# An attention and two expert layers on one core: the first pair's hash projections and first scores in smaller operations, and a new order

## The chip, the core and the metric

One core of a Trainium2 chip runs one program. The metric is the device time of one execution in microseconds (us), shown as the median of a few runs. The engines are TensorE (PE; its weight loads are PEld), VectorE (DVE), ScalarE (ACT), GpSimd (POOL) and SyncE (SP), which only issues DMAs. Each engine takes its instructions in the order in which they stand in its own queue.

## What is computed

The reference is an attention with hashed masks (batch 2, 8 heads, 768 positions, 64 columns per head), whose output passes through two feed-forward networks without any routing.

```
q_bits = (q @ proj > 0); k_bits = (k @ proj > 0)        # six bits each
mask   = bucket(q_bits) == bucket(k_bits)
scores = where(mask, q @ k.T / 8, -1e9)
attn   = exp(scores - max) / (sum + 1e-9);  x = attn @ v
h = x @ w_in;   x = (h * sigmoid(h)) @ w_out            # 1536 x 512 -> 2048 -> 512
a = x @ w1; b = x @ w2;  out = ((a * b) @ w3) @ wo2     # 512 -> 1024 -> 1024 -> 512
```

## The kernel before

The 16 heads are worked off as eight pairs, each pair on 128 partitions (one head on each half). For a pair the kernel multiplies the transposed q and k by the hash matrix (the projections), turns the results into sign bits on VectorE, and adds the bits to the scores as a fourth product with a large weight, so that entries outside the bucket fall far below the others. For each block of 128 rows of a head it then takes the row's peak on VectorE, the exponential on ScalarE, transposes the probabilities, and multiplies them with V. Meanwhile the weights of the two networks are loaded as split words, joined, and divided into a rounded part and a rest ("pieces", helper `piece`); three matmuls of such parts stand for one of full precision. The product of w3 and wo2 (L961) is made during the attention too. After the attention come the layers' matmuls (L1124, L1244, L1288).

The first pair is made in another way than the others (`lone` in the code). Its q and k arrive in four quarters of 384 columns (`raw["k", 0]` and so on, L540). Each is rounded (helper `scaled`, L348 to L352) and the rest is taken by a subtraction (`rest`, L592 on VectorE, L355 on POOL). The projections (`project`, L623) and signs (`sign`, L629) are made per half of the columns, q and k together; the weighted marks of k (`mark_k`, L679) follow, one operation per half. The scores (`scores_lone`, L767) of one block of rows of both heads are one operation of four passes:

```
passes = [("qhi", "khi"), ("qlo", "khi"), ("qhi", "klo"), ("bits", "marks")]
for p, (x, y) in enumerate(passes):
    ...
    for g in range(2):
        for side in range(2):
            ...
            nc.tensor.matmul(out=area(side * NQ + i)[:, g, :HF], lhsT=lhs[k, qs],
                             rhs=rhs[k, g * HF:g * HF + HF], start=(p == 0), stop=(p == 3))
```

Peaks of all pairs are L771, exponentials L777. The first pair's probabilities are turned by TensorE (L800), moved into their tile (`carry`, L806 on ScalarE or L808 on VectorE), and summed up with V (L842); the other pairs' are turned by VectorE (L818) and weighed by L876, and their scores are L755. At a pair's end the rows' sums are raised (L906, POOL or VectorE), inverted (L910, VectorE) and turned (L913). L535 are filler matmuls, whose result nobody reads.

What stands in which engine's queue is not left to a scheduler. Every operation is recorded with its possible engines, its predecessors and the buffers that it takes and gives back. Two tables at the head of the file then set everything: `ORDER` lists the operations' numbers in the order in which they are issued, and `ON` has a letter for the engine of each (P, A, D, G, S).

```
for n, e in zip(ORDER, ON):
    o = self.ops[n]
    ...
    for pool, key in o.take:
        self.held[key] = pool, self.free[pool].pop(0)
    o.emit(ENGINES[e])
```

Buffers are taken from their pools in this order, so an order also decides which buffer an operation gets. The costs and due times that the calls of `op` carry are not used when the program is built.

Of the kernel before, what the change touches and what calls it, by code (L numbers as in the profile page):

```python
# [12 lines left out]
ALU = mybir.AluOpType  # L13
# [215 lines left out]
def dve(n):  # L229
    return (n + 72) / 0.96  # L230
# [33 lines left out]
class Plan:  # L264
# [10 lines left out]
    def op(self, on, emit, deps=(), due=0.0, take=(), give=(), size=0, port=False, kind=None, tiled=False):  # L275


        self.ops.append(Op(on, emit, deps, take, give))
        return self.ops[-1]
# [1132 lines left out]
```

## Time and profile before

| what | us |
|---|---|
| median of 3 runs | 693.67 |
| lowest and highest run | 688.51, 696.32 |
| the profiled execution | 689.96 |
| its span, first to last instruction | 688.2 |
| TensorE busy in it | 668.1 |
| VectorE, ScalarE, POOL busy | 517.4, 381.5, 259.5 |

The profile is one execution. A busy engine is not always a fast one: the granted clock (PEclk) says at which share of full speed TensorE was let run. In rows of instructions the first figures are the start and the duration in us, and the square bracket names how long the engine stood idle before it and what ended that.

### The profile page before, as it was taken

What the parts mean: (1) busy time and instruction counts of PE and PEld (TensorE: products, weight loads), DVE (VectorE), ACT (ScalarE), POOL (GpSimd) and SP (SyncE); (2) the same over time, 40 slices, a digit from 0 to 9 for tenths busy, and PEclk for the clock granted to TensorE, in tenths of its full rate; (3) what the DMA queues carried; (4) which work ended last, traced back from release to release, by engine and by line L of the source; (5) the groups of instructions that cost most, each with busy time, mean ns of one, the idle gap of its engine ahead of it and who ended that gap; (6) DMA issues with size and microseconds to landing.
All of it is one profiled execution on the core that took longest, in us unless ns stands there. A gap on an engine that the chain in (4) does not pass through costs nothing.

```text
span 688.2 us, 13741 instructions
## 1 busy us (share of the span) xinstructions
PE 668.1 (97%) x5542; PEld 544.8 (79%) x5542; DVE 517.4 (75%) x736; ACT 381.5 (55%) x707; POOL 259.5 (38%) x268
## 2 busy tenths in 40 slices
PE   8899999998998998999999999999999999999997
PEld 6557787877787887888888888888887788888886
DVE  5889989978899867667796976778868575545465
ACT  5788778757778665467653543643545454322220
POOL 5468986777686220674200220211223144000000
PEclk9899999999999999999999999999999999999999
DMA  6465665446435444012530121110310012000004
GB/s 198 132 216 156 205 169 159 140 134 209 129 104 133 116 105 129 1 61 63 177 129 1 61 92 47 61 47 1 122 47 28 20 61 77 1 0 16 0 16 168
DMA packets 21551, 64.16 MB, mean 93 GB/s; under 512 B 3312, under 2 KB 4848, under 8 KB 21040
## 3 DMA queue, kind: packets, MB, share of 16 engines
q1 hardware_dynamic: 21488, 63.30, 29.8%
q8 instruction: 43, 0.70, 0.4%
q14 instruction: 20, 0.16, 0.1%
HBM read 55.19 MB, written 5.29 MB: 88 GB/s over the span
## 4 chain that ended last, share of the span: by engine, by line
PE 86%; DVE 6%; ACT 3%; issue 3%; DMA 1%; SPq 0%; ACTq 0%; DVEq 0%
PE more L1288 20%; PE more L1124 16%; PE more L1244 9%; PE acc L1288 9%; PE score L755 7%; PE acc L876 5%; PE acc L961 5%; PE acc L1124 4%; PE acc L1244 4%; DVE st L771 2%; PE turn L876 2%; ACT P L777 2%; PE acc L842 1%; PE score L767 1%; DVE pt L818 1%
## 5 line engine op out<-in xcount | busy, mean ns | idle before, releaser
L1124 PE MATMUL more<-y,piece 128*128 128x512 f32 x498 | 126.3, 390 | 0.6 <-DVE y L355 0.3
L1124 PEld LDWEIGHTS more<-y,piece 128*128 128x128 f32 x498 | 93.0, 188 | 21.7 <-DVE y L355 0.8
L777 ACT ACTIVATE P<-score,st 128x768 f32<-128x768 f32 x92 | 82.6, 899 | 37.4 <-DVE st L771 33.0
L771 DVE TENSOR_REDUCE st<-score 128x1 f32<-128x770 f32 x92 | 85.5, 943 | 13.1 <-PE score L755 10.1
L1288 PE MATMUL more<-gh,piece 128*128 128x512 f32 x256 | 88.5, 390 | 0.0
L818 DVE STREAM_TRANSPOSE pt<-P 128x768 f32<-128x768 f32 x84 | 79.9, 963 | 4.9 <-ACT P L777 4.7
L1307 DVE SCALAR_TENSOR_TENSOR X<-more,X 128x512 f32<-128x512 f32 x84 | 57.0, 686 | 35.0 <-PE more L1288 34.6
L1244 PE MATMUL more<-x,piece 128*128 128x512 f32 x252 | 65.1, 390 | 0.0
L876 PE MATMUL turn<-pt,V 32*64 32x193 f32 x1344 | 61.0, 325 | 3.3 <-issue 3.3
L876 PE MATMUL acc<-pt,V 32*64 32x193 f32 x1344 | 60.9, 325 | 2.4 <-issue 1.7
L876 PEld LDWEIGHTS acc<-pt,V 32*64 32x64 f32 x1344 | 50.5, 130 | 7.5 <-issue 6.2
L1288 PEld LDWEIGHTS more<-gh,piece 128*128 128x128 f32 x256 | 48.1, 188 | 10.2 <-DVE kraw L1190 0.3
L1244 PEld LDWEIGHTS more<-x,piece 128*128 128x128 f32 x252 | 47.2, 188 | 10.1 <-DVE X L1307 0.3
L755 PE MATMUL score<-ka,qa 128*128 128x384 f32 x168 | 46.9, 360 | 4.4 <-ACT P L777 4.3
L876 PEld LDWEIGHTS turn<-pt,V 32*64 32x64 f32 x1344 | 47.0, 130 | 4.6 <-issue 4.6
L352 POOL TENSOR_SCALAR piece<-x 128x512 fp32r<-128x512 f32 x35 | 24.1, 691 | 70.6 <-PE more L1288 29.4
L961 PE MATMUL acc<-piece,piece 128*128 128x512 f32 x192 | 50.1, 397 | 0.0
L1288 PE MATMUL more<-gl,piece 128*128 128x512 f32 x128 | 49.8, 389 | 0.0
L405 DVE SCALAR_TENSOR_TENSOR x<-x,x 128x512 uint32<-128x512 uint32 x57 | 43.3, 762 | 3.0 <-ACT x L390 2.3
L755 PE MATMUL score<-kb,qb 76*128 76x384 f32 x168 | 43.3, 338 | 0.0
L755 PEld LDWEIGHTS score<-ka,qa 128*128 128x128 f32 x168 | 28.3, 188 | 17.5 <-ACT P L777 9.5
L1288 PE MATMUL more<-piece,gh 128*128 128x512 f32 x132 | 40.6, 389 | 0.0
(229 smaller groups left out, 1426.1 us busy)
## 6 DMA issues: line engine op xcount, KB each, us to landing
raw<-in_w SPq DMA_DIRECT2D x27, 512.0 KB
raw<-in_wo SPq DMA_DIRECT2D x21, 512.0 KB
raw<-in_win SPq DMA_DIRECT2D x15, 512.0 KB
V<-in_v SPq DMA_DIRECT2D x14, 384.0 KB
invb<-inverse SPq DMA_DIRECT2D x16, 192.0 KB
out<-X SPq DMA_DIRECT2D x11, 256.0 KB
qraw<-in_qT SPq DMA_DIRECT2D x7, 384.0 KB
kraw<-in_kT SPq DMA_DIRECT2D x7, 384.0 KB
```

Source lines behind the costliest of these rows:

```text
L352: engine[e].tensor_scalar(out=dst, in0=src, scalar1=by, scalar2=1.0, op0=ALU.mult, op1=ALU.mult)
L405: engine[e].scalar_tensor_tensor(out=u32(x), in0=u32(x), scalar=3, in1=u32(t), op0=ALU.logical_shift_left, op1=ALU.bitwise_or)
L755: nc.tensor.matmul(out=sc[:, g, :HF], lhsT=lhs[:k, qs], rhs=rhs[:k, g * HF:g * HF + HF], start=(k == 128), stop=(k != 128),)
L771: nc.vector.tensor_reduce(out=plan[uk("st")][:, 0:1], in_=area()[:, :, :HF + 1], op=ALU.max, axis=AX.XY, negate=True)
L777: nc.scalar.activation(out=plan[uk("P")], in_=area()[:, :, :HF], func=AF.Exp, bias=s[:, 0:1], accum_out=plan[key("sums")][:, par * NQ + i: ...
L818: nc.vector.transpose(plan[mine][:, :, 32 * i:32 * i + 32], plan[uk("P")].rearrange("p g (b i) -> p (g b) i", i=32))
L876: nc.tensor.matmul(out=to[a][64 * side:64 * side + 64, :GW + 1], lhsT=V[rows_, c, side], rhs=plan[key(f"pt{side}")][rows_, c, :GW + 1], st ...
L961: nc.tensor.matmul(out=plan[key + ("ps",)], lhsT=w[:, a, k], rhs=r[:, c], start=(k == 0 and n == 0), stop=(k == 7 and n == 2),)
L1124: nc.tensor.matmul(out=plan[bk[b]], lhsT=w[:, a], rhs=y, start=(opens and j == 0 and m == 0), stop=(j == 1 and m == 2), skip_group_check=True)
L1244: nc.tensor.matmul(out=plan[key], lhsT=w[:, a], rhs=x, start=(k == 0 and n == 0), stop=(k == 3 and n == 2))
L1288: nc.tensor.matmul(out=plan[key], lhsT=a, rhs=x, start=(f == 0 and n == 0), stop=(f == 1 and n == 2))
L1307: nc.vector.scalar_tensor_tensor(out=dst, in0=plan[key], scalar=by, in1=dst, op0=ALU.mult, op1=ALU.add)
```

## The change

The first pair's projections are now made per half of the columns and per source: k's two matmul calls, then q's two, each with a sign operation on its own 64 partitions, in place of one projection of four calls and one sign on 128 partitions. The marks of k wait for k's sign alone. The first scores (block 0 of both heads) are two operations: three passes that wait for the rounded parts and rests, and the marked pass, which waits for the marks and for q's sign; the other blocks' scores wait for q's sign too. 2,939 recorded operations become 2,944. `ORDER` and `ON` are new as a whole; numbered alike, their last 1,307 entries are the same as before.

```
 SOON = 60
 ORDER = [
-    32, 34, 36, 35, 33, 44, 40, 38, 42, 827, 841, 0, 37, 18, 19, 1, 46, 48, 14, 13, 45, 39, 43, 47, 49, 51, 52, 54, 55,
+    32, 34, 33, 36, 35, 832, 846, 0, 37, 17, 1, 42, 43, 44, 40, 833, 834, 835, 46, 30, 50, 10, 52, 4, 45, 38, 39, 41, 47,
...
-            def project(e, f=f, fs=fs, key=key):
-                for t in range(4):
-                    nc.tensor.matmul(
-                        out=plan[key(f"z{f}")][32 * t:32 * t + 32, :HF], lhsT=ptl[:, t % 2],
-                        rhs=plan[key("qk"[t // 2] + "raw")][:, fs], start=True, stop=True,
-                    )
...
+            for w, nm in enumerate("kq"):
+                rows_ = slice(64 - 64 * w, 128 - 64 * w)
+
+                def project(e, f=f, fs=fs, nm=nm, key=key):
+                    for t in (0, 1) if nm == "q" else (2, 3):
+                        nc.tensor.matmul(
+                            out=plan[key(f"z{f}")][32 * t:32 * t + 32, :HF], lhsT=ptl[:, t % 2],
+                            rhs=plan[key(nm + "raw")][:, fs], start=True, stop=True,
+                        )
+
+                def sign(e, f=f, fs=fs, rows_=rows_, key=key, of_pair=part_of_pair):
+                    nc.vector.tensor_scalar(
+                        out=of_pair("bits")[rows_, fs], in0=plan[key(f"z{f}")][rows_, :HF], scalar1=0.0, scalar2=sel[rows_, 0:1],
+                        op0=ALU.is_gt, op1=ALU.is_equal,
                     )
...
-                    mine.append(op({"DVE": 420, "POOL": pool1(HF)}, mark_k, [signs[f], *mine], -5,
+                    mine.append(op({"DVE": 420, "POOL": pool1(HF)}, mark_k, [signs[2 * f], *mine], -5,
...
-                def scores_lone(e, key=key, i=i, qs=qs, of_pair=part_of_pair, area=area):
+                def scores_lone(e, key=key, i=i, qs=qs, of_pair=part_of_pair, area=area, of=range(4)):
                     passes = [("qhi", "khi"), ("qlo", "khi"), ("qhi", "klo"), ("bits", "marks")]
                     for p, (x, y) in enumerate(passes):
+                        if p not in of:
+                            continue
...
+                    if lone and i == 0:
+                        part = op({"PE": 0.75 * ns}, lambda e, f=scores_lone: f(e, of=range(3)), halves_in, tu - 3, areas, kind="scores_most")
+                        sc = both[i] = op({"PE": 0.25 * ns}, lambda e, f=scores_lone: f(e, of=(3,)), [part, *marked], tu - 3, kind="scores_last")
+                    else:
+                        sc = both[i] = op({"PE": ns}, scores_lone if lone else scores, [*marked, *halves_in], tu - 3, areas)
```

Three places show what the new order makes of the queues. In these rows a line number is that of the kernel in question (L623 and L629 are now L626 and L632, L771 is L775, L808 is L817), a tile's name carries a running number, and "waits" names whose progress an instruction waits for (PE, DVE, Pool, Activation, or one of the DMA queues DMAHW).

The first place is TensorE's queue at the start of the program, before the change and then after it. The tile turn holds the projections, ptl the hash matrix, score the first scores, ident is the fillers' operand.

```order
4 L623 MATMUL turn_81<-qraw_103,ptl 32x384 [waits DMAHW2_49,Pool_49]
5 L623 MATMUL turn_81<-qraw_103,ptl 32x384 [waits Pool_49]
6 L623 MATMUL turn_81<-kraw_104,ptl 32x384 [waits DMAHW3_49]
7 L623 MATMUL turn_81<-kraw_104,ptl 32x384
8 L623 MATMUL turn_81<-qraw_103,ptl 32x384 [waits DMAHW1_49]
9 L623 MATMUL turn_81<-qraw_103,ptl 32x384
10 L623 MATMUL turn_81<-kraw_104,ptl 32x384 [waits DMAHW0_49]
11 L623 MATMUL turn_81<-kraw_104,ptl 32x384
12 L535 MATMUL acc_80<-ident 128x128 x6
13 L767 MATMUL score_82<-x_98 128x384 [waits Activation_49]
```

The same queue after the change:

```order
4 L626 MATMUL turn_81<-kraw_104,ptl 32x384 [waits DMAHW1_49,DVE_49]
5 L626 MATMUL turn_81<-kraw_104,ptl 32x384 [waits DVE_49]
6 L535 MATMUL turn_81<-ident 128x128 x3
7 L626 MATMUL turn_81<-kraw_104,ptl 32x384 [waits DMAHW0_49]
8 L626 MATMUL turn_81<-kraw_104,ptl 32x384
9 L535 MATMUL acc_80<-ident 128x128 x3
10 L626 MATMUL turn_81<-qraw_103,ptl 32x384 [waits DMAHW2_49]
11 L626 MATMUL turn_81<-qraw_103,ptl 32x384
12 L535 MATMUL acc_80<-ident 128x128 x3
13 L626 MATMUL turn_81<-qraw_103,ptl 32x384 [waits DMAHW3_49,DVE_49]
14 L626 MATMUL turn_81<-qraw_103,ptl 32x384
15 L771 MATMUL score_82<-x_98 128x384
```

Both projections of k now stand ahead of both of q, with fillers between them, and the last one of q waits for VectorE, where before it no projection did.

The second place is VectorE's queue up to the first peak (st), before and then after. The tile x holds the rounded parts, the rests and the bits, invb the marks; x_93 to x_96 are words of weights that are joined.

```order
7 L592 SCALAR_TENSOR_TENSOR x_98<-kraw_104,x_98 128x384 [waits DMAHW0_49,Activation_49]
8 L592 SCALAR_TENSOR_TENSOR x_98<-qraw_103,x_98 128x384 [waits DMAHW2_49,Activation_49]
9 L629 TENSOR_SCALAR x_98<-turn_81,kraw_104 128x384 [waits DVE_49,PE_49]
10 L629 TENSOR_SCALAR x_98<-turn_81,kraw_104 128x384
11 L679 TENSOR_SCALAR invb_128<-x_98,kraw_104 44x384 [waits DVE_49]
12 L592 SCALAR_TENSOR_TENSOR x_98<-qraw_103,x_98 128x384 [waits DMAHW1_49]
13 L405 SCALAR_TENSOR_TENSOR x_93<-x_93,x_94 128x512 [waits Activation_49]
14 L771 TENSOR_REDUCE st_119<-score_82 128x1 [waits PE_49]
```

The same queue after the change, from the first rounding on (the four copies of the hash matrix stand ahead of it):

```order
10 L350 CAST x_98<-kraw_104 128x384 [waits DMAHW1_49]
11 L592 SCALAR_TENSOR_TENSOR x_98<-kraw_104,x_98 128x384 [waits DVE_49]
12 L592 SCALAR_TENSOR_TENSOR x_98<-kraw_104,x_98 128x384 [waits Activation_49]
13 L352 TENSOR_SCALAR x_98<-qraw_103 128x384 [waits DMAHW3_49]
14 L592 SCALAR_TENSOR_TENSOR x_98<-qraw_103,x_98 128x384 [waits DVE_49]
15 L592 SCALAR_TENSOR_TENSOR x_98<-qraw_103,x_98 128x384 [waits DMAHW2_49,Activation_49]
16 L632 TENSOR_SCALAR x_98<-turn_81,kraw_104 64x384 [waits PE_49] x2
17 L632 TENSOR_SCALAR x_98<-turn_81,kraw_104 64x384
18 L681 TENSOR_SCALAR invb_128<-x_98,kraw_104 44x384 [waits DVE_49]
19 L405 SCALAR_TENSOR_TENSOR x_93<-x_93,x_94 128x512 [waits Activation_49]
20 L632 TENSOR_SCALAR x_98<-turn_81,kraw_104 64x384
21 L775 TENSOR_REDUCE st_119<-score_82 128x1 [waits PE_49]
```

Two roundings and a subtraction have come to this queue from ScalarE and POOL, the signs are four, of which the first two wait for TensorE each, and one stands behind the join.

The third place is VectorE's queue from the first pair's third peak to that of its fourth block of rows, before and then after. The tile pt takes the moved probabilities, bits the second pair's signs.

```order
16 L771 TENSOR_REDUCE st_121<-turn_81 128x1
17 L808 TENSOR_SCALAR pt_126<-score_82 128x6x128
18 L771 TENSOR_REDUCE st_122<-acc_80 128x1
19 L808 TENSOR_SCALAR pt_126<-turn_81 128x6x128
20 L771 TENSOR_REDUCE st_119<-score_83 128x1
21 L771 TENSOR_REDUCE st_120<-score_82 128x1
22 L808 TENSOR_SCALAR pt_125<-acc_80 128x6x128
23 L610 TENSOR_SCALAR bits_108<-turn_81,kraw_104 128x384
24 L808 TENSOR_SCALAR pt_126<-score_83 128x6x128
25 L405 SCALAR_TENSOR_TENSOR x_93<-x_93,x_95 128x512
26 L808 TENSOR_SCALAR pt_125<-score_82 128x6x128
27 L771 TENSOR_REDUCE st_121<-acc_80 128x1
```

The same stretch after the change:

```order
20 L775 TENSOR_REDUCE st_121<-turn_81 128x1
21 L817 TENSOR_SCALAR pt_126<-score_82 128x6x128
22 L775 TENSOR_REDUCE st_122<-acc_80 128x1
23 L775 TENSOR_REDUCE st_119<-score_83 128x1
24 L775 TENSOR_REDUCE st_120<-score_82 128x1
25 L817 TENSOR_SCALAR pt_125<-acc_80 128x6x128
26 L610 TENSOR_SCALAR bits_108<-turn_81,kraw_104 128x384
27 L405 SCALAR_TENSOR_TENSOR x_95<-x_95,x_93 128x512
28 L817 TENSOR_SCALAR pt_125<-score_82 128x6x128
29 L775 TENSOR_REDUCE st_121<-acc_80 128x1
```

Five moves are three here; the two others are ScalarE's now.

## Rows read from the trace of the kernel before

**Rows 1.** Busy us (instructions) of each engine by stretch, then granted clock, DMA share, GB/s.

```profile
0.00:45.00 45.00, 39.73 (x261) 27.22 (x263) 32.01 (x47) 31.65 (x56) 23.13 (x34) 0.92 0.55 175
45.00:265.00 220.00, 209.77 (x3453) 173.84 (x3449) 191.21 (x238) 162.40 (x316) 145.85 (x133) 1.00 0.51 150
265.00:310.00 45.00, 44.69 (x189) 36.43 (x190) 33.31 (x54) 25.86 (x50) 25.36 (x26) 0.96 0.14 47
310.00:688.00 378.00, 373.89 (x1643) 307.33 (x1641) 260.90 (x400) 161.63 (x290) 65.15 (x77) 1.00 0.17 56
sum 688.00, PE 668.08 PEld 544.82 DVE 517.43 ACT 381.54 POOL 259.50; mean PE 167.02 PEld 136.21 DVE 129.36 ACT 95.39 POOL 64.87
```

**Rows 2.** Timeline of the first 13 us: start, duration, engine, instruction.

```profile
5.51 0.52 ACT L348 ACTIVATE x<-qraw 128x384 fp32r<-128x384 f32 x1 [1.20 <-DMA qraw<-in_pair]
...
6.74 0.52 ACT L348 ACTIVATE x<-kraw 128x384 fp32r<-128x384 f32 x1 [0.71 <-DMA kraw<-in_pair]
...
7.43 0.82 PE L623 MATMUL turn<-kraw,ptl 128*32 128x384 f32 x4
...
8.29 1.14 DVE L629 TENSOR_SCALAR x<-turn,kraw 128x384 fp32r<-128x384 f32 x2 [1.67 <-PE turn L623]
...
9.47 0.42 DVE L679 TENSOR_SCALAR invb<-x,kraw 44x384 fp32r<-44x384 f32 x1
...
9.93 0.56 DVE L592 SCALAR_TENSOR_TENSOR x<-qraw,x 128x384 fp32r<-128x384 f32 x1
...
10.23 0.62 PE L767 MATMUL score<-invb,x 12*128 12x384 f32 x4
...
10.40 0.68 DVE L405 SCALAR_TENSOR_TENSOR x<-x,x 128x512 uint32<-128x512 uint32 x1
...
11.01 1.82 DVE L771 TENSOR_REDUCE st<-score 128x1 f32<-128x770 f32 x2
```

**Rows 3.** The same timeline, from 15 to 44 us.

```profile
15.81 0.87 PE L800 MATMUL turn<-ident,P 128*128 128x128 f32 x6 [1.02 <-ACT P L777]
...
25.73 0.94 DVE L771 TENSOR_REDUCE st<-acc 128x1 f32<-128x770 f32 x1
...
28.69 1.54 PE L800 MATMUL acc<-ident,P 128*128 128x128 f32 x6
...
30.34 0.96 DVE L808 TENSOR_SCALAR pt<-acc 128x768 f32<-128x768 f32 x1 [1.60 <-PE acc L800]
...
31.44 2.96 PE L842 MATMUL acc<-pt,V 128*64 128x384 f32 x12
...
38.55 2.16 PE L842 MATMUL acc<-pt,V 128*64 128x384 f32 x12
38.66 1.83 DVE L771 TENSOR_REDUCE st<-score 128x1 f32<-128x770 f32 x2 [1.12 <-PE score L767]
...
43.70 0.95 DVE L771 TENSOR_REDUCE st<-score 128x1 f32<-128x770 f32 x1
```

**Rows 4.** Groups by line and shape, VectorE and ScalarE: busy, mean ns, idle before.

```profile
L808 DVE TENSOR_SCALAR pt<-score 128x768 f32<-128x768 f32 x4 | 3.8, 946 | 1.6 <-PE score L800 1.6
L808 DVE TENSOR_SCALAR pt<-acc 128x768 f32<-128x768 f32 x2 | 1.9, 953 | 1.6 <-PE acc L800 1.6
L808 DVE TENSOR_SCALAR pt<-turn 128x768 f32<-128x768 f32 x1 | 1.0, 958 | 0.4 <-PE turn L800 0.4
...
L390 ACT ACTIVATE x<-raw 128x512 f32<-128x512 f32 x8 | 5.3, 660 | 0.0
L806 ACT ACTIVATE pt<-score 128x768 f32<-128x768 f32 x4 | 3.2, 809 | 0.2
```

**Rows 5.** Busy us of each engine and granted clock in single microseconds.

```profile
25.00:26.00 1.00, 0.14 (x2) 0.14 (x4) 1.00 (x2) 1.00 (x2) 0.00 (x0) 1.00 0.91 337
...
27.00:28.00 1.00, 1.00 (x7) 0.56 (x5) 1.00 (x2) 1.00 (x3) 0.00 (x0) 0.50 0.62 145
...
33.00:34.00 1.00, 1.00 (x8) 0.29 (x6) 0.70 (x2) 1.00 (x3) 0.22 (x1) 0.95 0.00 0
```

More of the change, by code (lines that the diff above doesn't have):

```diff
@@ L217 @@
[L217 to L221 removed]
+    "NSSSSSSDDPPDDAAAANPPPPPPDDDDDGPNDDDNPPDDDPDAANGSSSSDDGGGGGGGGGAAPAPPADDPDDAAAPPPDDAPAAANPDGGGDPDANAA"
@@ L222 @@
+    "PGAPGAAPDAPDDPDGPGPDGPGPGPPAAPNNDPGADPADPDPDNPDPDPDNPAPDNPPPPPPAPNADPDDPDPPAAPADPDPDPAPPPDPPPDPPDPPD"
+    "PDPPAPDPDPPPPDPADPNPNNDAPDAPDAPDDSPDPPPPPPDPPDPPPPPAPNNADPDAGDPADPDNPDNPNNDAPGDPDAPDAPDNAPADDPDPDPPP"
+    "APAAPDPDPDPPPPDPPPPPAPNDPDAPDPPPAPPDPDAPDPPPDPNAPDAPDDPDPADPDPAPPDPSPDPNNPDPDPNNDPDAPNNADPDPDDPDPDPN"
+    "DSPADSPDSPDPSPDPSPDPSPDPSPPNDDSDPSPSPDPNNSDS"
 )
@@ L619, in lsh_attention_moe_kernel @@
             fs = slice(f * HF, f * HF + HF)
-            def project(e, f=f, fs=fs, key=key):
-                for t in range(4):
-                    nc.tensor.matmul(
-                        out=plan[key(f"z{f}")][32 * t:32 * t + 32, :HF], lhsT=ptl[:, t % 2],
-                        rhs=plan[key("qk"[t // 2] + "raw")][:, fs], start=True, stop=True,
-                    )
-            def sign(e, f=f, fs=fs, key=key, of_pair=part_of_pair):
-                nc.vector.tensor_scalar(
-                    out=of_pair("bits")[:, fs], in0=plan[key(f"z{f}")][:, :HF], scalar1=0.0, scalar2=sel[:, 0:1],
-                    op0=ALU.is_gt, op1=ALU.is_equal,
-                )
-            p = op({"PE": 150 + 4 * (PE_FREE + HF * PE_COL)}, project, [raw["q", f], raw["k", f], placed_tiled], lead + 3 + f,
-                   [("R", key(f"z{f}"))], kind="project_lone")
-            zs.append(p)
-            signs.append(op({"DVE": dve(HF) + 60}, sign, [p, ls, *signs], lead + 7 + f,
-                            [("bits", key("bits"))] if f == 0 and not lone else [], [key(f"z{f}")]))
+            for w, nm in enumerate("kq"):
[10 more added lines that the diff above has]
+                        op0=ALU.is_gt, op1=ALU.is_equal,
+                    )
+                p = op({"PE": 720}, project, [raw[nm, f], placed_tiled, zs[-1] if w else None], lead + 3 + f,
+                       [] if w else [("R", key(f"z{f}"))], kind="project_half")
+                zs.append(p)
+                signs.append(op({"DVE": dve(HF) + 60}, sign, [p, ls, signs[-1] if w else None], lead + 7 + f, [], [key(f"z{f}")] if w else []))
         def weight(e, key=key):
@@ L784, in lsh_attention_moe_kernel @@
                 else:
-                    sc = both[i] = op({"PE": 500 + 8 * (PE_FREE + HF * PE_COL) if lone else 4 * (PE_FREE + HF * PE_COL)},
-                                      scores_lone if lone else scores,
-                                      [*gathers[par], *(x[y] for x in (hi, lo) for y in (("k", 0), ("k", 1), ("q", 2 * i // NQ)) if lone)], tu - 3,
-                                      [(p, (x, "u", v)) for v, q in (((u, "R"), (u + NQ, "W")) if lone else ((u, "S"),))
-                                       for p, x in ([(q, ("S", y)) for y in range(2)] if lent_out else [("S", "S")])])
+                    halves_in = [x[y] for x in (hi, lo) for y in (("k", 0), ("k", 1), ("q", 2 * i // NQ)) if lone]
+                    marked = [*gathers[par], *([signs[2 * (2 * i // NQ) + 1]] if lone else [])]
+                    areas = [(p, (x, "u", v)) for v, q in (((u, "R"), (u + NQ, "W")) if lone else ((u, "S"),))
+                             for p, x in ([(q, ("S", y)) for y in range(2)] if lent_out else [("S", "S")])]
+                    ns = 500 + 8 * (PE_FREE + HF * PE_COL) if lone else 4 * (PE_FREE + HF * PE_COL)
+                    if lone and i == 0:
[3 more added lines that the diff above has]
+                        sc = both[i] = op({"PE": ns}, scores_lone if lone else scores, [*marked, *halves_in], tu - 3, areas)
                 scored.append(sc)
```

55 lines of the change are left out of this document (25 added, 30 removed), and 289 rows, old and new, of the table ORDER.

## Prediction

> **What bounds the kernel now.** I read the busy times by stretch first [rows 1]. TensorE is busy 668.08 of 688 us, VectorE 517.43. From 310 us on TensorE works 373.89 of 378 us, from 45 to 265 us it works 209.77 of 220, and in the first 45 us only 39.73, at a mean granted clock of 0.92. So its idle time is 5.3 us before 45, 10.2 between 45 and 265, 0.3 to 310 and 4.1 after. The change is written into the first 45 us, so I read that stretch as a timeline next. There TensorE is not what ends last: its first scores end, VectorE takes their peaks from 11.01 [rows 2], and from then on VectorE goes from one instruction to the next: the peaks of the fourth block of rows begin at 25.73, those of the sixth at 38.66, the first one of the second pair at 43.70 [rows 3]. What bounds this stretch is VectorE's in-order queue and what it waits for.
>
> **The start: projections, signs, first scores.** Four quarters of the first pair arrive one after the other; ScalarE starts on the third at 5.51 and on the fourth at 6.74 [rows 2]. They were issued as k, q, q, k and now as k, k, q, q, at about equal sizes, so I take it that the fourth is now the half of q which the first scores need, at the same 6.74. The scores' three passes can then start without the marks, but they do not set the time: the first peak needs the marked pass, and nearly all the work for that after 6.74 is VectorE's, in the order that the second place of the section on the change shows. Before, ScalarE made all four roundings, and POOL the copies and one of the four subtractions; now VectorE makes two roundings, the copies and all four subtractions.
>
> Step by step from 6.74. Rounding that half of q: 0.42 (not shown on this engine; the nearest row is the marking operation on 384 columns, 0.42; the ends are 0.28, half of a subtraction, and 0.57, a sign). Two subtractions at 0.56. The first sign at 0.57, as two took 1.14 [rows 2]. That is 8.85. Here stands a wait that is new: in the order the last q projection waits for VectorE and the next sign for TensorE, where before all four projections ended ahead of the first sign. The projection costs 0.82 [rows 2], and I add 0.1 for two handovers (before, the sign began 0.04 after the projection's end): 9.77. Queued behind on VectorE are two signs, the marking and a join, 0.57 + 0.57 + 0.42 + 0.68 = 2.24 [rows 2], and one more sign of 0.57 that stands ahead of the first peak: 12.58. A sign on 64 partitions I cost like one on 128, as it has as many columns; half of that is the lower end. The marked pass (0.62 [rows 2]) starts after the marking, at about 11.4, and hides behind the join and the fourth sign; without that cover its 0.62 would be added. **First peak: 12.6 against 11.01, 1.6 us later** (ends: +0.1, if the projection doesn't wait and signs cost half; +2.3, if the rounding takes 0.57 and each handover 0.3 more). TensorE itself has the same eight projection calls as before, in four groups instead of two: no cost.
>
> **The rest of the first pair.** Of the twelve moves of turned probabilities VectorE makes 7 before, at 0.95, and 5 after; the two that go to ScalarE cost 0.81 each there [rows 4]. The third place shows VectorE up to the fourth block's peak: from the first peak it takes 14.72 us before (25.73 − 11.01), and now has two moves fewer. So that peak comes at 12.58 + 14.72 − 1.90 = 25.4, 0.3 earlier than before: the late start is paid back, if ScalarE (31.65 of 45 us busy [rows 1]) has room for 1.6 us. If it has none, this is 0 and the 1.6 stays.
>
> Then the clock. In the slice at 25 us TensorE is busy 0.14 and the granted clock is 1.00; at 27 it is 0.50, the lower of its two levels, 1.2 GHz; at 33 it is 0.95 [rows 5]. In between a set of turns takes 1.54 where one at 2.4 GHz takes 0.87, and the summing 2.96 against 2.16 [rows 3]: with two sets that is 2 × 0.67 + 0.80 = 2.1 us, and VectorE idles 1.60 before its move there [rows 3], so I put it all on the path to the sixth block's peaks. In the new order TensorE issues the scores of two blocks back to back and then two sets of turns, ahead of the place where it idled; I take it that the clock doesn't fall there. Of the 2.1 I give 0.7 back, for a filler and a summing (2.16) that now stand ahead of the next block's turns. The sixth block's peaks then come at 38.66 − 0.3 − 1.4 = 37.0. From there: two peaks to 38.9, exponential to 39.9, then on ScalarE move, conversion and move, 0.81 + 0.66 + 0.81 [rows 4], to 42.2, scores of the second pair about 1.0, first peak of the second pair at 43.3 against 43.70. It reads the bank that is freed second, where before it read the one freed first. **Term: −0.4** (ends: −2.4, if that bank doesn't matter; +1.7, if the clock falls as before).
>
> The Trainium skill speaks against counting on the clock: "TensorE: Matmul & The Clock Gate", Part 1, says that the window of the clock's monitor runs free of the kernel's start, so that the place of a change differs between runs. By that rule part of the 2.1 belongs to this one execution and not to its order, and the term would lie between −0.4 and +1.7 whatever the order is. One execution can't decide that.
>
> **A new wait at the pair's end.** The sums' floor is now raised on POOL instead of VectorE. In POOL's queue a conversion stands ahead of it that waits for the VectorE instruction just before the reciprocal. So VectorE waits for two POOL instructions: one like ScalarE's conversion, 0.66 [rows 4], and one on 12 columns, which I put between nothing and 0.66: some 1.1 with handovers. Behind the reciprocal stand two joins and the second pair's first peak. I cost it at nothing, because the reciprocal begins at about 40.8 and the joins (1.4) end ahead of the bank's scores at 43.3; without that cover it is +1.1.
>
> **From 45 us on.** To 310 the same instructions stand in another order, a few on other engines. Removing all idle time of TensorE between 45 and 265 would give −10.2; as much again would cost +10.2 [rows 1]. I take 0: counted in the order, 192 combining matmuls and 72 and 24 early ones of the first layers' two products stand ahead of the last pair's sums in both. From 265 to 310 the mean granted clock is 0.96 [rows 1], so 45 × 0.04 = 1.8 us are lost there, which may go or double. The last 1,307 operations are issued in the same order by the same engines: 0.
>
> **Sum.** At 43 us +1.6 − 1.9 − 0.1 = −0.4, and 0 from there: 689.96 − 0.4 = 689.6 for the profiled execution, whose span is 688.2 with 1.76 around it. That execution lies 3.7 below the median of the three runs, 693.67, so the median becomes 693.3. The runs spread from 688.51 to 696.32; about 1%, 6.9 us, is what a measurement of this kernel tells from no change.
>
> **Rivals.**
> 1. *The first scores do come early.* If the fourth quarter lands sooner, or the half signs cost half, the first peak comes at 10.5 instead of 12.6, and the pair's end gains 2.0 more: 691.3. For it: 6.74 is one arrival, with other loads beside it. Against: nine VectorE instructions stand between that arrival and the first peak.
> 2. *Faster by the new order at large.* The clock's losses go (2.1 and 1.8) and with them two fifths of the 10.2 us of idle time (4.1): 693.67 − 8.0 = 685.7. For it: that idle time lies in a stretch where VectorE has 191.21 of 220 us [rows 1] and some room. Against: TensorE has as many matmuls ahead of the last pair's sums as before, so nothing says that they fill its pauses better.
> 3. *Slower: the clock falls at the start.* TensorE's last projection now waits from about 7.5 to 8.9 for a sign, and the marked pass from 11 to 11.4. If the clock falls for these pauses and once more behind them, with the old fall kept, each new fall costs like the old one, 2.1 and with the scores in it some 2.9: 2 × 2.9 on top of the late start's 1.6 is 693.67 + 7.4 = 701.1. It decides when the clock is at 0.50 in three stretches ahead of 45 us; with one it is +1.7. Against: the clock stays up before 25 us now, though TensorE pauses there too (39.73 of 45 [rows 1]).
>
> **How the numbers follow.** Forecast 0.50, rival 1 0.20, rival 2 0.16, rival 3 0.14. The first two lie within 1%: same 0.70; faster by over 1% 0.16; slower by over 1% 0.14. The range takes in the two outer rivals, and with them half of the idle time either way: 685 to 701.
>
> **What would show it.** The last q projection begins after the first sign ends; the first peak stands at about 12.6; VectorE makes five moves; the clock stays at 1.00 from 26 to 33; the second pair's first peak lies within 1 us of 43.3. A first peak before 11.0, or under 6 or over 15 us of idle TensorE between 45 and 265, makes the reasons wrong even if the time is right.

## The result, and the profile after

| | before | changed |
|---|---|---|
| median (20 runs each) | 689.35 | 693.85 |
| lowest and highest | 687.12, 696.32 | 689.31, 697.98 |
| the profiled execution | 689.96 | 692.90 |
| its span | 688.2 | 691.1 |

The changed kernel is slower: ratio 1.0056, 95% interval 1.0029 to 1.0082, which is 2.0 to 5.7 us. Ratios and intervals, here and below, leave out the few executions that lie over 1.5% above the fastest of their kernel; medians are of all. The forecast was 693.3, inside 685 to 701, and 0.4 us under the kernel before. So the time is nearly the one that was named, and the direction is wrong: 17 more runs of the kernel before moved its median from 693.67 to 689.35, next to the execution that had been profiled.

The first thing to read is the busy time by stretch again, as [rows 1] but cut finer. Before the change, from 45 us on (columns as there):

```profile
45.00:180.00 135.00, 128.94 (x2038) 105.45 (x2034) 119.97 (x150) 100.39 (x196) 103.36 (x96) 1.00 0.56 167
180.00:260.00 80.00, 77.37 (x1288) 65.62 (x1285) 69.83 (x86) 59.20 (x116) 42.49 (x38) 1.00 0.43 121
260.00:290.00 30.00, 28.16 (x252) 22.89 (x237) 20.77 (x35) 16.05 (x31) 10.44 (x10) 0.94 0.19 60
290.00:310.00 20.00, 20.00 (x89) 16.30 (x89) 13.95 (x22) 12.62 (x25) 14.92 (x16) 1.00 0.16 53
```

The same view of the changed kernel, with the first 45 us, which answer to the first row of [rows 1]:

```profile
0.00:45.00 45.00, 39.50 (x270) 25.64 (x272) 31.24 (x52) 29.24 (x51) 25.93 (x35) 1.00 0.56 179
45.00:180.00 135.00, 129.92 (x2024) 104.99 (x2020) 118.54 (x149) 101.01 (x195) 99.28 (x94) 1.00 0.60 167
180.00:260.00 80.00, 75.66 (x1158) 62.42 (x1165) 66.44 (x85) 60.92 (x118) 42.26 (x36) 1.00 0.39 113
260.00:290.00 30.00, 28.71 (x378) 23.99 (x363) 24.18 (x36) 16.71 (x33) 11.99 (x13) 1.00 0.26 82
290.00:310.00 20.00, 18.65 (x83) 15.05 (x82) 16.71 (x24) 11.26 (x22) 6.94 (x6) 1.00 0.14 44
```

In the first 45 us TensorE idles 5.50 us (5.27 before), at a granted clock of 1.00 instead of 0.92. From 180 to 260 it idles 4.34 instead of 2.63, and from 290 to 310 it idles 1.35, where before it did not idle at all.

The start, as a timeline; these rows answer to [rows 2]:

```profile
5.18 1.14 PE L626 MATMUL turn<-kraw,ptl 128*32 128x384 f32 x4
...
6.25 0.55 PE L535 MATMUL turn<-ident 128*128 128x128 f32 x3
...
6.73 0.84 PE L626 MATMUL turn<-kraw,ptl 128*32 128x384 f32 x4
...
7.50 0.55 PE L535 MATMUL acc<-ident 128*128 128x128 f32 x3
...
7.97 0.84 PE L626 MATMUL turn<-qraw,ptl 128*32 128x384 f32 x4
...
8.86 0.62 DVE L632 TENSOR_SCALAR x<-turn,kraw 64x384 fp32r<-64x384 f32 x1 [0.90 <-PE turn L626]
...
9.54 0.84 PE L626 MATMUL turn<-qraw,ptl 128*32 128x384 f32 x4 [0.25 <-DVE x L632]
...
10.43 1.26 DVE L632 TENSOR_SCALAR x<-turn,kraw 64x384 fp32r<-64x384 f32 x2 [0.94 <-PE turn L626]
...
11.84 0.80 PE L771 MATMUL score<-invb,x 12*128 12x384 f32 x4 [0.20 <-DVE x L632]
12.17 0.69 DVE L405 SCALAR_TENSOR_TENSOR x<-x,x 128x512 uint32<-128x512 uint32 x1
...
12.78 0.60 DVE L632 TENSOR_SCALAR x<-turn,kraw 64x384 fp32r<-64x384 f32 x1
...
13.31 1.81 DVE L775 TENSOR_REDUCE st<-score 128x1 f32<-128x770 f32 x2
```

The first peak comes at 13.31 (before 11.01). VectorE waits 0.90 for TensorE, then TensorE for VectorE, then VectorE 0.94 for TensorE: that is the new wait between the last q projection and the signs. From there on, in rows that answer to [rows 3]:

```profile
26.47 0.94 DVE L775 TENSOR_REDUCE st<-acc 128x1 f32<-128x770 f32 x1
...
38.20 1.83 DVE L775 TENSOR_REDUCE st<-score 128x1 f32<-128x770 f32 x2 [1.14 <-PE score L771]
...
42.42 0.23 DVE L919 RECIPROCAL sums<-sums 128x12 f32<-128x12 f32 x1 [1.09 <-POOL sums L915]
42.57 1.22 DVE L405 SCALAR_TENSOR_TENSOR x<-x,x 128x512 uint32<-128x512 uint32 x2
44.35 1.83 DVE L775 TENSOR_REDUCE st<-score 128x1 f32<-128x770 f32 x2 [0.56 <-PE score L757]
```

2.30 late at the first peak, 0.74 late at the fourth block (25.73 before), 0.46 early at the sixth (38.66), 0.65 late at the second pair (43.70). In this execution most of the late start was paid back, by fewer moves on VectorE and by the clock, which stays up where it fell before:

```profile
27.00:28.00 1.00, 1.00 (x14) 0.75 (x12) 1.00 (x2) 0.49 (x1) 0.90 (x2) 1.00 0.89 340
...
33.00:34.00 1.00, 1.00 (x8) 0.43 (x5) 0.38 (x1) 0.83 (x2) 0.92 (x2) 1.00 0.94 290
```

The loss between 290 and 310 us has one place. In the list of TensorE's waits these two stand among the first; the second was not there before:

```profile
PE score L757 <- ACT P L781: 2.7, 6, 0.9
...
PE more L1133 <- DVE X L1316: 1.3, 1, 1.3
```

Its timeline, where X<-more is the move that empties a bank:

```profile
293.96 1.52 PE L1133 MATMUL more<-y,piece 128*128 128x512 f32 x6
294.35 1.82 DVE L355 TENSOR_TENSOR y<-X,y 128x512 fp32r<-128x512 f32 x2
...
296.09 0.68 DVE L1316 SCALAR_TENSOR_TENSOR X<-more,X 128x512 f32<-128x512 f32 x1
...
296.83 1.43 PE L1133 MATMUL more<-y,piece 128*128 128x512 f32 x5 [1.35 <-DVE X L1316]
```

### The profile page after: what moved, and what is told of

Its sections match the earlier page's. It is cut to its first block, busy times and chain, and to the rows that moved or that the text cites. A ratio compares the mean times of both kernels' runs of the same rounds, so it can differ in the third digit from the quotient of the medians.

```text
span 691.1 us, 13738 instructions
## 1 busy us (share of the span) xinstructions
PE 669.1 (97%) x5542; PEld 541.3 (78%) x5542; DVE 520.6 (75%) x747; ACT 383.4 (55%) x708; POOL 251.9 (36%) x257
## 4 chain that ended last, share of the span: by engine, by line
PE 82%; DVE 7%; ACT 6%; issue 3%; DMA 1%; POOL 0%; ACTq 0%; DVEq 0%; POOLq 0%
PE more L1297 21%; PE more L1133 15%; PE more L1253 7%; PE score L757 7%; PE acc L885 7%; PE acc L1297 7%; PE acc L1253 4%; PE acc L1133 4%; PE acc L970 4%; ACT P L781 2%; PE turn L885 2%; DVE st L775 2%; DVE gl L355 1%; DVE y L355 1%; DVE x L405 1%
## 5 line engine op out<-in xcount | busy, mean ns | idle before, releaser
L775 DVE TENSOR_REDUCE st<-score 128x1 f32<-128x770 f32 x92 | 85.4, 944 | 19.0 <-PE score L757 13.9
L1297 PE MATMUL more<-gh,piece 128*128 128x512 f32 x272 | 94.8, 389 | 0.0
L1316 DVE SCALAR_TENSOR_TENSOR X<-more,X 128x512 f32<-128x512 f32 x96 | 65.2, 688 | 37.8 <-PE more L1297 37.6
L885 PE MATMUL acc<-pt,V 32*64 32x193 f32 x1344 | 62.6, 325 | 4.5 <-issue 3.9
L1253 PE MATMUL more<-x,piece 128*128 128x512 f32 x240 | 61.3, 390 | 0.0
L1297 PEld LDWEIGHTS more<-gh,piece 128*128 128x128 f32 x272 | 51.1, 188 | 10.8 <-DVE X L1316 0.2
L1297 PE MATMUL more<-gl,piece 128*128 128x512 f32 x136 | 52.9, 389 | 0.0
L1253 PEld LDWEIGHTS more<-x,piece 128*128 128x128 f32 x240 | 45.0, 188 | 9.6 <-DVE X L1316 0.3
L405 DVE SCALAR_TENSOR_TENSOR x<-x,x 128x512 uint32<-128x512 uint32 x55 | 40.4, 739 | 14.0 <-ACT x L390 13.1
L348 ACT ACTIVATE sg<-more 128x512 f32<-128x512 f32 x31 | 18.4, 595 | 52.4 <-PE more L1133 43.5
L1297 PE MATMUL more<-piece,gh 128*128 128x512 f32 x152 | 46.8, 389 | 0.0
```

The costliest lines, as they stand in the source:

```text
L405: engine[e].scalar_tensor_tensor(out=u32(x), in0=u32(x), scalar=3, in1=u32(t), op0=ALU.logical_shift_left, op1=ALU.bitwise_or)
L775: nc.vector.tensor_reduce(out=plan[uk("st")][:, 0:1], in_=area()[:, :, :HF + 1], op=ALU.max, axis=AX.XY, negate=True)
L885: nc.tensor.matmul(out=to[a][64 * side:64 * side + 64, :GW + 1], lhsT=V[rows_, c, side], rhs=plan[key(f"pt{side}")][rows_, c, :GW + 1], st ...
L1253: nc.tensor.matmul(out=plan[key], lhsT=w[:, a], rhs=x, start=(k == 0 and n == 0), stop=(k == 3 and n == 2))
L1297: nc.tensor.matmul(out=plan[key], lhsT=a, rhs=x, start=(f == 0 and n == 0), stop=(f == 1 and n == 2))
L1316: nc.vector.scalar_tensor_tensor(out=dst, in0=plan[key], scalar=by, in1=dst, op0=ALU.mult, op1=ALU.add)
```

## The experiments

Theory 1: the later first peak passes through to the end. Theory 2: the new order behind the first pair costs. Theory 3, a rival: the split itself costs, through the waits on the tile that its projections share. OLD and NEW are the two order tables, with the numbers and engine letters of each entry; "then" means the rest in the other table's order. Cuts are counted with the five entries that only the split has: in a kernel without it five fewer stand ahead of the cut. "Before" is always the kernel before, run beside it on the same chip.

**The split and the order apart.** First the changed functions in the old order:

```diff
-ORDER = NEW
+ORDER = OLD, with 46, 47, 50, 51, 59 right ahead of 48, 49, 52, 53, 60
```

> The changed kernel's operations (split projections, signs and first scores) in the order and on the engines of the kernel before; each new operation stands directly ahead of the one it was split from. Theory 1 (the later first peak passes through to the end): four signs of 0.60 in place of two of 0.57 put the first peak some 1.2 us later than 11.0, so 0 to 1.5 us over the kernel before, a ratio of 1.000 to 1.002. Theory 2 (what costs is the new order behind the first pair): no difference, 1.000. Theory 3 (the split itself costs, through the waits on the shared tile): 1.004 to 1.006.

Measured: 692.42, ratio 1.0016 (0.9987 to 1.0045). Four signs stand in one row, 2.56 us for all, and the first peak is at 12.28. Theory 1 foretold this time; the interval ends where theory 3 begins and takes in no difference as well. Then the unsplit functions in the new order:

```diff
 # functions of the kernel before
-ORDER = OLD
+ORDER = NEW without 46, 47, 50, 51, 59; both signs and marks behind 48
```

> The operations of the kernel before (no split) in the order and on the engines of the changed kernel; both signs stand where the sign of q's first half stood. Theory 1: VectorE's roundings stay ahead of the signs, so the first peak is at about 12 to 12.5 and the time 1 to 3 us over the kernel before, 1.002 to 1.004. Theory 2: the whole loss, 1.005 to 1.006. Theory 3 (the split): 1.000.

Measured: 692.19, 1.0031 (0.9999 to 1.0062). The first peak is at 10.60, earlier than before and 2.7 earlier than with the split: for the first peak the new load order and VectorE's roundings are good, the split is not. Yet the time is not lower than before, so something behind the start costs.

**Start and rest crossed.**

```diff
-ORDER = NEW
+ORDER = NEW[:160] then OLD
```

> The changed kernel's first 160 entries of the order (to about 35 us), and everything behind them in the order and on the engines of the kernel before. Theory 1: first peak at 13.3 as in the changed kernel, and the whole loss, 1.004 to 1.006. Theory 2: 1.000 to 1.001.

Measured: 692.32, 1.0045 (1.0010 to 1.0079).

```diff
-ORDER = OLD
+ORDER = OLD[:158] then NEW
```

> The kernel before for its first 158 entries of the order (to about 35 us, no split), and everything behind them in the order and on the engines of the changed kernel. Theory 1: first peak at 11.0 and no loss, 0.998 to 1.001. Theory 2: the whole loss, 1.004 to 1.006.

Measured: 696.31, 1.0081 (1.0055 to 1.0107), with the first peak at 11.11. Theory 1 foretold no loss here, theory 2 none in the run above: neither holds alone.

**A late start by itself.**

```diff
             def sign(e, f=f, fs=fs, key=key, of_pair=part_of_pair):
-                nc.vector.tensor_scalar(
+                for _ in range(3):
+                    nc.vector.tensor_scalar(
```

> The kernel before, with each of the first pair's two sign operations made three times (the same result): four more VectorE instructions of 0.57 us ahead of the first peak, which comes at 13.3 instead of 11.0, and nothing else is changed. Theory 1 (a later first peak passes through to the end): 1.5 to 3 us over the kernel before, 1.002 to 1.0045. Rival (later waits absorb it): 1.000 to 1.001.

Measured: 695.70, 1.0062 (1.0034 to 1.0090): 2.3 to 6.2 us for a first peak at 13.46. In this profile the clock falls in two stretches, of which one microsecond each is shown:

```profile
15.00:16.00 1.00, 1.00 (x5) 0.56 (x6) 1.00 (x2) 1.00 (x3) 0.66 (x1) 0.50 1.04 366
32.00:33.00 1.00, 1.00 (x7) 1.00 (x6) 0.47 (x1) 1.00 (x3) 0.96 (x1) 0.50 0.84 280
```

So a late start is not free, and the clock behind TensorE's pauses may be most of its price: the mean granted clock over the ten executions is 0.9880, against 0.9932 in the kernel before. As an estimate, with all the time bound by TensorE, that is 690 × 0.0052 = 3.6 of the 4.3 us.

**The new start without the split.**

```diff
 # functions of the kernel before
-ORDER = OLD
+ORDER = NEW[:160] as in the unsplit run above, then OLD
```

> The unsplit operations in the changed kernel's order to about 35 us, then the order and the engines of the kernel before. First peak at about 10.6. Theory A (start and rest cost separately, and add up): without the late start and without the new rest, 0 to 2 us under the kernel before, 0.997 to 1.000. Theory B (any change of the start costs, since the rest was fitted to the old one): 1.002 to 1.005.

Measured: 688.85, 0.9966 (0.9938 to 0.9994). Theory B is excluded. The time is theory A's, but that the two costs add up is not shown: 3.1 us (new start, old rest) and 5.6 (old start, new rest) would make 8.7, and the changed kernel lost 3.9. The kernel is 2.3 us faster than the one before, and its mean granted clock is 0.9980 against 0.9932: by the same estimate 3.3 us, so the gain is no larger than what the clock gives. The same cut at 885 entries:

```diff
-ORDER = OLD
+ORDER = NEW[:885] as in the unsplit run above, then OLD
```

> The unsplit operations in the changed kernel's order to about 180 us, then the order and the engines of the kernel before. First peak at 10.6, no pause at 297 us. Theory C: the late start and the two costs behind 180 us are all gone, so 1 to 4 us under the kernel before, 0.994 to 0.999. Rival (the new order costs ahead of 180 us too): 1.000 to 1.004.

Measured: 688.76, 0.9982 (0.9957 to 1.0007), no pause at 297 us: up to 180 us the new order costs nothing that shows. (Here too the mean granted clock is higher, 0.9965 against 0.9937, by the estimate 1.9 us; a cost of that size could hide behind it.)

**Where the new order costs.** The old table up to a cut, the new one behind it:

```diff
-ORDER = OLD
+ORDER = OLD[:415] then NEW      # 90 us
+ORDER = OLD[:886] then NEW      # 180 us
+ORDER = OLD[:1071] then NEW     # 87 of 96 peaks
+ORDER = OLD[:1211] then NEW     # 260 us
```

> The kernel before for its first 415 entries of the order (to about 90 us: two pairs finished), and everything behind them in the order and on the engines of the changed kernel. If what the new order costs behind the first pair lies before 90 us: 1.000 to 1.001. If it lies behind: 1.003 to 1.006.

Measured: 695.05, 1.0073 (1.0047 to 1.0098).

> The kernel before for its first 886 entries of the order (to about 180 us: five pairs finished), and everything behind them in the order and on the engines of the changed kernel. If what the new order costs lies before 180 us: 1.000 to 1.001. If it lies in the last pairs and the first layers' part before 310 us (the pause of 1.35 at 296.8): 1.002 to 1.005.

Measured: 694.64, 1.0074 (1.0041 to 1.0107).

> The kernel before for its first 1,071 entries of the order (to about 215 us: six pairs finished and 87 of the 96 blocks' peaks taken), and everything behind them as in the changed kernel. If most of the loss between 180 and 260 us lies behind 215 us: 1.004 to 1.007. If it lies between 180 and 215 us: 1.000 to 1.002.

Measured: 691.99, 1.0015 (0.9985 to 1.0046). The 88th peak stands at 223 us in this profile, so the cut is some 8 us later than its expectation says.

> The kernel before for its first 1,211 entries of the order (to about 260 us: the attention's last sums), and everything behind them in the order and on the engines of the changed kernel. If the two costs behind 180 us are separate: only the pause at 297 us is left, 1.0 to 1.8 us over the kernel before, 1.0015 to 1.0026, and TensorE loses as little between 180 and 240 us as in the kernel before. If the whole loss lies behind 260 us: 1.005 to 1.007.

Measured: 690.41, 1.0005 (0.9984 to 1.0025), with the pause of 1.51 before 296 us in its profile. So, with the old start, the loss lies between 180 and about 223 us for the most part. The stretches of this kernel and of the one cut at 180 us, one below the other:

```profile
180.00:260.00 80.00, 77.42 (x1312) 66.07 (x1319) 69.33 (x86) 59.96 (x117) 42.29 (x38) 1.00 0.43 122
```
```profile
180.00:260.00 80.00, 75.27 (x1251) 63.20 (x1255) 64.38 (x84) 59.34 (x114) 40.46 (x34) 1.00 0.41 116
```

2.58 us of idle TensorE with the old order there, 4.73 with the new one.

**The changed kernel, mended in one place each.** The order behind 180 us undone:

```diff
-ORDER = NEW
+ORDER = NEW[:885] then OLD
```

> The changed kernel for its first 885 entries of the order (to about 180 us: five pairs finished), and everything behind them in the order and on the engines of the kernel before. Theory C (of what the change costs, some 3 us lie between 180 and 240 us and 1.5 us in the pause at 297 us, and the late start costs the rest): the pause at 297 us is gone and TensorE waits less between 180 and 240 us, so 3 to 4 us under the changed kernel, 0.999 to 1.002 of the kernel before. Rival (the new order behind 180 us only costs when it follows the old order): as the changed kernel, 1.005 to 1.006.

Measured: 692.18, 1.0041 (1.0016 to 1.0067): between theory C (0.999 to 1.002) and its rival (1.005 to 1.006), and the interval reaches both. The trace does what theory C said: no pause at 297 us, and as little lost time behind 180 us as with the old order (8.25 in the table below). The time does not follow by a clear amount: 1.0 us under the changed kernel's 3.9.

```diff
-ON: 1634, 1638, 1649, 1652, 1656, 1658 on D
+ON: the same on G
```

> The changed kernel with five subtractions (the rests of the first layers' inputs, at 290 to 300 us) and one folding sum back from VectorE to POOL, as they were before; the order is unchanged. If TensorE's pause of 1.35 at 296.8 us comes from these on VectorE ahead of the move that frees its bank: the pause is gone, and the time 1.0 to 1.5 us under the changed kernel, 1.0035 to 1.0045 of the kernel before. Rival (POOL is then late with the rests and TensorE waits for these): a pause of 1 us or more stays within 290 to 305 us, and no gain.

Measured: 694.28, 1.0055 (1.0027 to 1.0082). The rival's outcome, though not for its reason: a pause of 1.21 stays ahead of 296 us, still behind the same move of VectorE, whose instructions ahead of it, now beside POOL's, take 1.78 instead of 0.68:

```profile
292.08 1.78 DVE L334 TENSOR_TENSOR piece<-sum,piece 128x512 fp32r<-128x512 f32 x1
293.78 1.78 DVE L334 TENSOR_TENSOR y<-X,y 128x512 fp32r<-128x512 f32 x1
295.49 0.68 DVE L1295 SCALAR_TENSOR_TENSOR X<-more,X 128x512 f32<-128x512 f32 x1
```

```diff
-46, 30, 50, 10, 52, 4, 45, 38, 39, 41, 47, 55, 48, 57, 51, 49, 56, 58, 59, 60,
+46, 50, 52, 45, 38, 39, 41, 48, 47, 55, 57, 51, 49, 56, 58, 59, 60, 10, 4,
```

> The changed kernel with all four half projections of the first pair issued one behind the other on TensorE, ahead of the first sign, and the three sets of fillers that stood between them moved behind the first scores (two) and to about 20 us (one). Then no projection waits for a sign. The first sign begins at about 8.9 and the first peak at 12.3 to 12.6 instead of 13.3. Theory 1 (the start passes through): 0.7 to 1 us under the changed kernel, 1.003 to 1.0045 of the kernel before. Rival (without fillers the clock falls): a stretch at a granted clock of 0.50 ahead of 45 us, and no gain.

Measured: 692.18, 1.0029 (1.0002 to 1.0057). The three signs stand in one row now, and the first peak is at 11.54, better than expected:

```profile
8.12 1.80 DVE L611 TENSOR_SCALAR x<-turn,kraw 64x384 fp32r<-64x384 f32 x3
...
11.54 1.81 DVE L754 TENSOR_REDUCE st<-score 128x1 f32<-128x770 f32 x2
```

(Entry 30, the third set of fillers, stands ahead of entry 26 there.) So the fillers between the projections and the wait for the sign made 1.8 us of the 2.3. The clock does not fall ahead of 45 us in this profile, as the rival would have it. The time is theory 1's, but its interval takes in the changed kernel's 1.0056.

```diff
-1733, 1734, 1745, 1133, 1134, 1657, 1783, 1654, 1658, 1735, 1656,
+1733, 1734, 1735, 1745, 1133, 1134, 1657, 1783, 1654, 1658, 1656,
```

> The changed kernel, with the one VectorE move that frees TensorE's bank at 296 us issued three instructions sooner, ahead of one rest of a sum and two rests of the first layers' inputs (0.7 + 1.8 us of VectorE's time). If the order of VectorE's queue makes the pause at 297 us: the pause of 1.35 is gone and the time is 1.0 to 1.4 us under the changed kernel, 1.0035 to 1.0045 of the kernel before. Rival (the rests are then late instead): a pause of about 1 us within 295 to 305 us stays, and no gain.

Measured: 696.39, 1.0096 (1.0064 to 1.0128), no gain. The pause moves on to the rests, as the rival said, only later, from 305 us on:

```profile
306.69 1.43 PE L1112 MATMUL more<-y,piece 128*128 128x512 f32 x5 [1.72 <-DVE y L334]
```

```diff
-ON behind entry 885: the engines of NEW
+ON behind entry 885: the engines of OLD (38 operations)
```

> The changed kernel in its own order, with the 38 operations behind 180 us whose engine had changed put back on the engines of the kernel before. If the loss behind 180 us comes from work that went to another engine (roundings and copies on ScalarE ahead of the exponentials that free the banks of the scores): TensorE loses 2 to 3 us less between 180 and 240 us, and the time is 2 to 4 us under the changed kernel, 1.000 to 1.003 of the kernel before. Rival (the order of the queues alone): as the changed kernel or slower, 1.005 to 1.008.

Measured: 698.96, 1.0105 (1.0062 to 1.0149). No gain: the engines that changed are not by themselves what costs behind 180 us. TensorE loses more there than in the changed kernel (13.86 against 11.08 in the table below); by the times the two intervals overlap. The other half, the old order on the new engines, was not tried.

**All profiles in one measure.** Idle time counts only gaps. To count a slow pace too, I subtracted from a moment's time the nominal duration of all matmuls that had begun by then (0.2265 us for 512 columns, 0.1745 for a score matmul, 0.109 for 128 columns, 0.0875 or 0.044 where two or four stand side by side, 0.0205 for V's 193 columns; the distances from start to start in unbroken stretches of the two traces). What is left is TensorE's lost time. All kernels issue the same matmuls, 5,542 in each trace. In us, by stretch:

```
                             first peak  to 45   180-260  290-310
before                           11.01   19.96     8.12     0.20
changed                          13.31   19.24    11.08     1.66
e1   split, old order            12.28   19.54     8.00     0.20
e2   unsplit, new order          10.60   20.05    10.33     1.66
e3   new start, old rest         13.33   18.89     8.51     0.22
e4   old start, new rest         11.11   18.48    10.86     1.74
e5   signs three times           13.46   22.45     8.22     0.15
e6   unsplit start, old rest     11.31   17.51     8.09     0.18
e7   old to 90, new rest         10.86   19.38    10.90     1.63
e8   old to 180, new rest        10.53   19.85    10.78     1.52
e9   new to 180, old rest        13.20   19.15     8.25     0.17
e10  rests on POOL               13.34   19.28    10.30     1.54
e11  start mended                11.54   18.37    11.25     1.48
e12  unsplit to 180, old rest    10.32   17.28     8.39     0.16
e13  move sooner                 12.65   21.71    10.09     2.03
e14  old to 260, new rest        10.42   19.73     7.59     1.88
e15  old engines behind 180      13.01   21.83    13.86     1.58
e16  old to 223, new rest        10.72   18.86     8.49     1.86
```

From 180 to 260 us the old order loses 7.6 to 8.5 in eight profiles, the new one 10.1 to 11.3 in eight: the means are 8.15 and 10.70, a difference of 2.55. From 290 to 310 it is 0.2 against 1.5 to 2.0, a difference of 1.5. Two kernels stand outside these groups and fit: the one cut at 223 us loses like the old order, and the one with mixed engines loses most. (In e12 and e16 a pause of 1.1 and 1.7 us lies across 260 us and is not in the third column.)

The idle gaps alone say what 1.6 of these 2.55 us are (the rest is a slower pace without a gap). Between 180 and 260 us they sum to 2.67 in the mean of the eight profiles with the old order and to 4.25 in the other eight. The waits for ScalarE's exponentials make 1.8 and 2.1 of that; gaps that end with no releaser in the profile ("issue"), nearly all between two of V's small matmuls, make 0.1 and 1.7. So the difference in idle time lies in these gaps. TensorE's waits in that stretch, first in the kernel cut at 260 us (old order there), then in the one cut at 180 us:

```profile
PE score L734 <- ACT P L756: 1.8, 2, 1.2
PE acc L855 <- ACT X L327: 0.7, 1, 0.7
```
```profile
PE acc L855 <- issue: 1.7, 2, 1.5
PE score L734 <- ACT P L756: 1.5, 2, 0.9
PE turn L855 <- issue: 0.9, 2, 0.4
PE acc L855 <- ACT X L327: 0.6, 1, 0.6
```

## Why the prediction was wrong

**Two terms of the sum failed.** The first is "From 45 us on ... I take 0". The same matmuls stand ahead of the last pair's sums in both orders, as the prediction counted, but that does not say that TensorE pauses as little: it loses 2.55 us more between 180 and 260, 1.5 more at 297 us. With the old start the new order behind 180 us cost 5.1 us (e8, at least 2.8). The range had room for it (plus or minus 10.2), the value taken had not. The second is the −0.4 at 43 us, the late start paid back: with the old order behind 35 or 180 us the changed start cost 3.1 and 2.8 us (e3, e9).

**The start, by its own steps.** The first sign was put at 8.28 (8.85 less one sign); it began at 8.86. The step "TensorE itself has the same eight projection calls: no cost" failed: its queue is full from 5.18 on, with a set of fillers ahead of every further projection, and q's second half is done at 8.81. The wait behind it was named and right, only larger: 10.43 instead of 9.77 for the second sign. A sign on 64 partitions takes 0.60 to 0.63, not less than one on 128 (0.57); the lower end, half of that, is out. VectorE itself was ready at 7.97, ahead of the forecast, and stood idle for 0.90. Together 13.31 instead of 12.58, and the mended start shows what made it late: 11.54 without fillers and wait. That the marked pass hides behind the join was right (11.84 to 12.64, peak at 13.31).

**The payback** was forecast at 1.9 by two moves fewer; the lateness fell from 2.30 to 0.74 by the fourth block, 1.56. The second pair's first peak came 0.65 late, not 0.4 early, at 44.35, 1.05 us from the forecast 43.3. The wait for POOL at the pair's end was forecast at 1.1, hidden: it is 1.09, VectorE then idles 0.56 for the scores, so it is hidden. The last 1,307 operations: 0 was right within what the profiles vary.

**The clock.** It stayed at 1.00 from 26 to 33 us in the changed kernel's profile, as forecast. But two kernels with the same start (e13, e15) show it at 0.50, its level of 1.2 GHz, from 28 or 29 us on, as in this row of the second:

```profile
30.00:31.00 1.00, 1.00 (x6) 0.56 (x5) 1.00 (x2) 0.92 (x3) 0.50 (x1) 0.50 0.77 166
```

So what one profile shows of the clock belongs in part to its execution: over all executions the mean granted clock is 0.9957 (20 of the changed kernel) against 0.9937 (34 of the kernel before, run beside the first experiments), by the estimate 690 × 0.0020 = 1.4 us for the order. The Trainium skill, "TensorE: Matmul & The Clock Gate", Part 1, says that the monitor's window runs free of the kernel's start; these profiles agree: a pause of 0.80 at 13 us is followed by a fall in these two, and one of 0.81 by none in the changed kernel.

**The sum as measured.** To 45 us, six profiles with the changed kernel's start lose 20.0 on average (changed, e3, e9, e10, e13, e15), six with the old start 19.4 (before, e4, e7, e8, e14, e16): 0.6. With 2.55 and 1.5 that is 4.6 us, against 3.9 measured (2.0 to 5.7). That the two agree is no proof: the sum leaves out the stretches from 45 to 180 us, where by the same measure the profiles lose between 17.7 and 25.1, and from 260 to 290 (4.4 before, 2.3 changed). Without the split (e2, e6, e12) the start loses 18.3. By the times, too, the split is dearer in the same order: 1.0045 against 0.9966 (e3, e6), 1.0041 against 0.9982 (e9, e12), 1.0056 against 1.0031 (changed, e2); a part of that is the clock (0.9948 against 0.9980 in the first two).

**What stays open.** The costs do not add up in the times. The changed start alone lost 3.1 and 2.8 us (e3, e9), where the sum gives 0.6; the new rest alone 5.6, 5.0 and 5.1 (e4, e7, e8), where it gives 4.1; the changed kernel has both and lost 3.9. So either cost is shown by itself, and which of the two the changed kernel pays for is not: undoing the rest gained 0.8 and 1.0 us (e3, e9), mending the start 1.9 (e11), none of it clear of noise; undoing the start gained nothing (e4, e8); and without the split and with the old order behind 180 us (e12) nothing was lost. The pause at 297 us costs 1.5 in every profile, while the kernel that has it alone (e14) lost 0.3, at most 1.7. Why TensorE pauses more between 180 and 260 us in the new order is open. Longer waits for ScalarE make 0.3 of it at most. The pauses stand at fixed counts of TensorE's instructions, as the last section shows, so an order decides which matmuls meet them; why they are long with one order and short with the other no run shows.

**The rivals.** The first (early first scores) did not happen; the second (faster by the order at large) is the reverse of what the order does; the third (the clock falls at the start) was seen in two of six starts, in two stretches each, at 2.6 us (21.8 lost to 45 us against 19.1 without it) where it put 5.8 for two falls.

**The baseline.** The median of three runs was taken as the level of the kernel before, 3.7 above the profiled execution. With 20 runs it is 689.35, and the profiled execution was the typical one. The forecast's 693.3 is near the measured 693.85 only because of that, by luck: from 689.35 the same −0.4 gives 689.0.

## What to carry to other kernels

Splitting this operation by partitions made no part cheaper on VectorE, and the parts, which share a tile with TensorE's outputs, waited for each other: unsplit, the same new start has its first peak 2.7 us earlier. With the old order behind it that kernel is at 0.9966 of the kernel before, a gain that the granted clock of its executions accounts for. When an order is replaced as a whole, equal counts of work ahead of a point are no reason for "no change": cross the two orders at a few points, see which stretch loses, and do not expect the losses to add up. And three runs that spread by 1% are no level to measure a change of 0.5% from.

## What the runs showed of the hardware

VectorE's subtraction on 128x512 took 0.68 alone and 1.78 beside POOL's, and four of POOL's took 6.67 us there, 1.67 each, against 1.30 where VectorE stood idle (before, at 298.81). The Trainium skill, "Trainium Architecture — The Big Picture", section "What this means for kernel authors", says that these two engines share a port under an exclusive lock; the rows agree that both are slower together.

TensorE shows pauses that wait for nothing the profile names, in the long runs of V's small matmuls: 1.69 at 142 us and 1.74 at 171 us before, 1.21 and 1.40 (at 175 us) after, up to 2.60 in other kernels. Their places are fixed by the instructions and not by the time. When all of TensorE's rows of a trace are counted from its start (matmuls, weight loads, 80 to 90 others), 106 of the 112 such pauses over 0.3 us behind 45 us, in the 18 traces, end at a count of 194 or 195 plus a multiple of 256: 3,522 and 4,290 before, 3,522 and 4,547 after. The other six, of 0.9 us, stand ahead of matmul 3,725 in six kernels with the old order there. The lengths differ between orders and from one execution to the next: 4,547 has a pause of 0.5 us or more in all ten kernels with the new order at that place, and none over 0.3 in the other eight.
